# Attention scores in four PSUM banks a head in place of six, maxima over fewer keys, and new due times, in a fused attention, Fourier and MLP kernel

## The chip, the cores and the metric

The kernel runs on one core of one Trainium2 chip. The metric is device time in microseconds of one execution; lower is better.

## The reference

There are 8 batches, 8 heads, 576 positions and 64 dimensions a head. Causal attention with a bias from a cumulative sum comes first, then a Fourier mixing over positions and features, a normalization, and an MLP with a residual:

```python
scores = scale * np.matmul(q, k.transpose(0, 1, 3, 2))
cum = np.cumsum(np.maximum(s, 0.0), axis=-1)
bias = -(cum[:, :, :, None] - cum[:, :, None, :])
scores = np.where(causal, -1000000000.0, scores + np.minimum(bias, 0.0))
attn = exp(scores - max(scores)); attn = attn / (sum(attn) + 1e-09)
x = (attn @ v)                                   # to (8, 576, 512)
u = x + real(fft(fft(x, axis=1), axis=2))
un = (u - mean(u)) / sqrt(var(u) + 1e-06)
out = u + np.maximum(un @ w_ch1, 0.0) @ w_ch2    # 512 -> 2048 -> 512
```

## The kernel before

**Stages.** Attention runs over 32 pairs of heads (8 batches, 4 pairs each; `pair`, `NP` = 32). After the four pairs of a batch its Fourier mixing follows (`folds`, `fourier`), interleaved with later pairs. In the same time the MLP's weights are converted. Then come the normalization and the MLP over nine tiles of 512 tokens: two in plain form (`mlp`), the others in a seven-product form (`fast_tile`, L347).

**One pair.** `high` copies q and k to a high part in the data type fp32r on ScalarE, `low` makes the low parts (VectorE and GpSimd). `maxes` finds each query's greatest score from the high parts alone and writes it as a row beside q, so that the scores' product subtracts it. `scores` makes the score blocks transposed, keys on partitions and queries in the free dimension. `av` multiplies with the values, and with ones for the sums; `recip` and `finish` normalize.

**Scores.** The keys are cut into five chunks of 128, 128, 128, 128 and 64 (`CH`). A key sees the queries from its own position on, so chunk c needs the queries from 128c: 576, 448, 320, 192 and 64 columns, 1600 in all, which lie side by side in the tile `P` (`POFF`, `PW` = 1984 with the unused end). Chunk 0 is cut in two (256 and 320 columns), and chunk 3 is computed over 256 columns, of which the exponential reads the last 192. So a head has six blocks of 256, 320, 448, 320, 256 and 64 columns. Each block (`one`) takes one of three PSUM banks (`ps`, `bufs=3`), gets two matmuls, one with the high parts (L684, `ky` and `qy`) and one with the parts for the correction (L685, `k1` and `q1`), each with its own weight load of 128 columns, and is read by one exponential on ScalarE (L690), which frees the bank. GpSimd then puts zeros above the diagonal: `select` (L709) for the first four chunks at once, behind their five exponentials (`diag`), and a small one (L697) for the fifth chunk, behind its own.

**Maxima.** `maxes` has eight steps a pair. `unit` is the form for the first two blocks of 128 queries: both heads side by side in one bank, 256 keys each (L588), then one bf16 matmul that adds the causal mask for both heads to the 128 columns at `cut` (L590), then one reduce on VectorE over the first `cut + 128` columns of each head (L593). `masked` (L600) and `last` (L624) take the other queries. Their banks are of another ring of three (`psm`).

**Order.** The program writes down each engine's order of instructions. The class `Flow` plans it when the kernel is built. Every piece of work is a generator that yields the engine that it wants next with an estimated cost, the events that it depends on and a ring's slot (a buffer). The planner simulates these engines, and among the pieces that could start within 0.02 us of the earliest it takes the one with the least due time. Due times come from the table `PR`: pair i is due at `D(i)`, which is `T * i` with T = 14.85 plus an offset `d<i>`, and the steps of a pair, the Fourier stages (`fold`, `fou`, `b<n>`, the last batch's `fo2`, `fo3`), the weights (`a0`, `dw`, `w2`, `lw`, `kp`) and the rest of the MLP (`c0`, `ld`) have offsets of their own. For instance the split of weight block f into two parts (L1087) is due at

```python
A0 = O + PR['a0']                        # O = T * 31 - 4
return A0 + 5.5 * f - PR['dw']           # due_w(f)
```

The planner's estimates only set the order; on the chip the engines wait for each other by semaphores.

Of the kernel before, what the change touches and what calls it, by code (L numbers as in the profile page):

```python
# [10 lines left out]
AF = mybir.ActivationFunctionType  # L11
# [18 lines left out]
N1 = 6  # L30
NW = 8
MARGIN = 1.5
PR = {'high': -1.74, 'hstep': 2.12, 'low': -1.84, 'p0': 0.0, 'p1': 0.0, 'p2': 0.0, 'p3': 0.0, 'win': 0.02, 'a0': 32.04, 'ld': 1.38, 'lw': 41.24, 'kp': 22.34, 'dw': 8.84, 'w2': 5.04, 'nf': -0.16, 'c0': 22.43, 'cvs': 7.29, 'lstep': 1.1, 'qs': -2.41, 'mx': -1.37, 'mxh': -6.12, 'mxc': 0.48, 'mt': 6.04, 'sc': -0.62, 'sch': 6.28, 'scs': 0.76, 'sel': 7.33, 'av': 10.36, 'avh': 15.59, 'avk': 4.5, 'rc': -1.89, 'fin': 17.87, 'fold': 4.62, 'fj': 5.3, 'fst': 2.33, 'fou': 7.67, 'gap': 3.41, 'fo2': 37.01, 'fo3': 43.31, 'gap2': 2.05, 'cv': -0.05, 'T': 14.85, 'b7': 5.15, 'd3': -2.77, 'd10': 4.59, 'd29': -1.01, 'd21': 6.35, 'd13': -0.31, 'b2': 0.88, 'd11': 0.25, 'd28': 0.04, 'b5': 0.6, 'd15': -6.3, 'd5': 3.97, 'd27': -0.16, 'd31': 0.19, 'd16': 2.45, 'd18': 1.56, 'd6': 3.13, 'd17': 0.55, 'd7': 0.12, 'd2': -0.15, 'd14': -3.6, 'd0': -1.05, 'd20': 1.74, 'b4': -3.07, 'd22': 3.32, 'd26': -1.87, 'b6': 9.14, 'd25': -1.62, 'b1': 0.96, 'd23': -1.21, 'd30': -4.22, 'd12': -3.32, 'd19': 1.36, 'd24': 4.33, 'd9': -0.04, 'b0': 0.58, 'd8': 0.46, 'd4': 2.24, 'b3': 0.22, 'd1': -0.58}
BACKLOG = 4.0


CH = [(128, 0, 576, 0), (128, 128, 448, 128), (128, 256, 320, 256), (128, 320, 256, 384), (128, 512, 64, 512)]
POFF = [0, 576, 1152, 1728, 1920]
# [4 lines left out]
def fused_kernel(ctx, tc, qkT, vA, sP, wP, tabD, tabS, corr, out):  # L43
    nc = tc.nc
# [6 lines left out]
    ps = ctx.enter_context(tc.tile_pool(name="ps", bufs=3, space=PSUM))  # L51
# [348 lines left out]
    psm = attp_ctx.enter_context(tc.tile_pool(name="psm", bufs=5, space=PSUM))  # L400
# [6 lines left out]
    flow = Flow()  # L407
    rings = {}

    def ring(name, n):  # L410
        if name not in rings:
            rings[name] = Ring(n)
        return rings[name]
# [3 lines left out]
    def ev(*name):  # L417
        return events.setdefault(name, Event())
# [3 lines left out]

    T = PR['T']

    def D(i):
        return T * i + PR.get('d%d' % i, 0.0)
# [144 lines left out]
    def maxes(i):  # L571
        st = sts[i]
        qy, ky = st["qy"], st["ky"]
# [5 lines left out]
        ready = [at(("rows", i), ("k", i, h), ("q", i, h)) for h in range(2)]  # L579

        def unit(c, k0, cut, out, done):


            e, hold = yield pe(2 * mm(256) + (0.0 if cut is None else 0.25), *ready[0], *ready[1], ring=(ring("psm", 3), 1))
            p = psm.tile([128, 512], F32, tag="m", name="pm", bufs=3)
            both = p.rearrange("p (h n) -> p h n", n=256)
            for h in range(2):
                nc.tensor.matmul(both[:, h], qy[:, h, 128 * c:128 * c + 128], ky[:, h, k0:k0 + 256], start=not h, stop=cut is None and h == 1, skip_group_check=True)  # L588
            if cut is not None:
                nc.tensor.matmul(both[:, :, cut:cut + 128], identb, mask2, start=False, stop=True, skip_group_check=True)  # L590
            valid = 256 if cut is None else cut + 128
            e = yield ("DVE", 0.16 + 0.00205 * valid, (e, *free), None)
            nc.vector.tensor_reduce(out=out, in_=both[:, :, 0:valid], axis=AX.X, op=ALU.max)  # L593
            hold.add(e)
            done.add(e)
# [47 lines left out]
        e, hold = yield pe(0.1, ev("max", i), ring=(ring("psm", 3), 1))  # L643
        p = psm.tile([128, 512], F32, tag="m", name="pmt", bufs=3)
        nc.tensor.transpose(out=p[0:9, 0:128], in_=M[:, 0:9], identity=ident)
        ev("moved", i).set(e)
        e, mthold = yield act(128, e, ring=(ring("mt", 2), 2))
# [13 lines left out]
        e = yield ("ACT", 0.74, (), None)  # L661
# [5 lines left out]
    def scores(i):  # L667
        st = sts[i]
        qy, ky, q1, k1 = st["qy"], st["ky"], st["q1"], st["k1"]
        st["P"], st["Phold"] = [], []  # L670
        scored = Last(ev("scored", i), 12)
        for h in range(2):
            _, hold = yield wait(ev("row", i), ev("low", i), ring=(ring("P", 4), 1))
            P = attp.tile([128, PW], F32, tag="P", name="P", bufs=4)
            st["P"].append(P)
            st["Phold"].append(hold)
            diag = Last(Event(), 5)

            def one(h, c, a, n, P, diag):
                nk, q0, nq, qk = CH[c]  # L680
                ksl = slice(128 * c, 128 * c + 128)
                e, hold = yield pe(2 * mm(max(n, 128)), ring=(ring("ps", 3), 1))
                p = bank("ps")
                nc.tensor.matmul(p[:, :n], ky[:, h, ksl], qy[:, h, a:a + n], start=True, stop=False)  # L684
                nc.tensor.matmul(p[:, :n], k1[:, h, ksl], q1[:, h, a:a + n], start=False, stop=True)  # L685
                scored.add(e)
                lo = max(a, qk)
                o = POFF[c] + lo - qk
                e = yield act(a + n - lo, e)
                nc.scalar.activation(P[:, o:o + a + n - lo], p[:, lo - a:n], AF.Exp, scale=0.125)  # L690
                hold.add(e)
                if c < 4:
                    diag.add(e)
                else:
                    e = yield pool_(64, e)
                    d5 = P[:, POFF[4]:POFF[4] + 64]
                    nc.gpsimd.affine_select(out=d5, in_=d5, pattern=[[1, 64]], compare_op=ALU.is_ge, fill=0.0, base=0, channel_multiplier=-1)  # L697
                    ev("P5", i, h).set(e)

            x = 0  # L700
            for c, (nk, q0, nq, qk) in enumerate(CH):
                for a, n in [(0, 256), (256, 320)] if c == 0 else [(q0, nq)]:
                    flow.add(one(h, c, a, n, P, diag), D(i) + PR['sc'] + PR['sch'] * h + PR['scs'] * x)
                    x += 1

            def select(P, diag, h):
                e = yield ("POOL", 0.68, (diag.event,), None)
                d4 = bass.AP(tensor=P.tensor, offset=P.offset, ap=[list(P.ap[0]), [576, 4], [1, 128]])
                nc.gpsimd.affine_select(out=d4, in_=d4, pattern=[[0, 4], [1, 128]], compare_op=ALU.is_ge, fill=0.0, base=0, channel_multiplier=-1)  # L709
                ev("P4", i, h).set(e)  # L710

            flow.add(select(P, diag, h), D(i) + PR['sch'] * h + PR['sel'])
        ev("begun", i).set(ev("row", i))
# [919 lines left out]
def pe(cost, *deps, ring=None):  # L1633
    return "PE", cost, deps, ring


def act(n, *deps, ring=None):
    return "ACT", 0.16 + n * 0.0009, deps, ring
# [26 lines left out]
def mm(n):  # L1665
    return 0.012 + n / 2350
# [146 lines left out]
```

## Time and profile before

| what | us |
|---|---|
| median of 3 runs | 1318.52 (1315.52 to 1319.11) |
| profiled execution, in all | 1313.49 |
| its span, first to last instruction | 1311.8 |
| TensorE busy in the span | 1235.9 |
| VectorE, ScalarE, GpSimd busy | 780.0, 607.2, 551.0 |
| granted TensorE clock, mean | 0.982 of full |

A matmul's row in the profile starts where the record puts it, and its end is modelled; it lasts longer than the time to the next start, because matmuls are pipelined. Weight loads are a row of their own (PEld) and overlap matmuls. A wait is put down to the operation that came last by the profile.

### The profile page before, as it was taken

The numbers are of one execution on the slowest core, as the hardware profiler recorded it, in microseconds if no ns is written. First come the engines' busy times: TensorE is split into PE (matmuls) and PEld (weight loads), VectorE is DVE, ScalarE is ACT, GpSimd is POOL, SyncE is SP. The second block draws the span as 40 slices with busy tenths as digits, with TensorE's granted clock in tenths as the row PEclk, the third lists the DMA queues.
The fourth block names the chain that finished last, engine by engine and source line by source line (L and its number), as shares of the span: only waits on it lengthen the run. The fifth ranks groups of instructions, "written<-read, shape, count | busy, mean of one in ns | idle before, by whom it ended". The sixth has DMA issues, their size and how long they took to land.

```text
span 1311.8 us, 22882 instructions
## 1 busy us (share of the span) xinstructions
PE 1235.9 (94%) x8414; PEld 1031.7 (79%) x8414; DVE 780.0 (59%) x1440; ACT 607.2 (46%) x1388; POOL 551.0 (42%) x569
## 2 busy tenths in 40 slices
PE   3998889899999979899999999999999999999998
PEld 2766667677776757787788888899888988888987
DVE  6566776847678577839757865444454444535323
ACT  2876776667676563425333432333233333333221
POOL 9456676857758675528743502102021021120100
PEclk9999899999999999999999999999999999999999
DMA  8867675646666465277543335244353442533433
GB/s 192 226 183 208 179 204 171 196 118 182 175 167 175 107 210 196 76 245 233 185 152 130 114 121 174 96 145 151 103 173 119 137 154 96 171 118 122 147 102 113
DMA packets 120395, 205.61 MB, mean 157 GB/s; under 512 B 16537, under 2 KB 38457, under 8 KB 120283
## 3 DMA queue, kind: packets, MB, share of 16 engines
q1 hardware_dynamic: 117707, 200.96, 49.1%
q0 software_dynamic: 1712, 2.53, 1.1%
q8 instruction: 66, 1.08, 0.3%
q10 hardware_dynamic: 864, 0.67, 0.2%
q14 instruction: 46, 0.38, 0.1%
HBM read 148.44 MB, written 31.72 MB: 137 GB/s over the span
## 4 chain that ended last, share of the span: by engine, by line
PE 55%; DVE 8%; POOL 3%; issue 3%; DMA 2%; ACT 1%; SPq 0%; POOLq 0%; DVEq 0%; ACTq 0%
PE b L347 20%; PE acc L259 7%; PE acc L258 7%; PE acc L260 7%; PE h L1396 4%; DVE we L88 1%; PE acc L1378 1%; PE acc L1377 1%; PE acc L1379 1%; DVE we L85 1%; PE pav L733 1%; PE pz L926 1%; DVE wl L1087 1%; PE pav L748 1%; DMA w2l<-wD 1%
## 5 line engine op out<-in xcount | busy, mean ns | idle before, releaser
L305 POOL TENSOR_TENSOR w<-w,o 128x512 f32<-128x512 f32 x28 | 37.2, 1338 | 346.5 <-DVE o L301 307.0
L259 PE MATMUL acc<-zh,w2l 128*128 128x512 f32 x452 | 179.3, 397 | 0.0
L258 PE MATMUL acc<-zh,w2h 128*128 128x512 f32 x452 | 178.8, 396 | 0.0
L260 PE MATMUL acc<-zl,w2h 128*128 128x512 f32 x452 | 177.2, 392 | 0.0
L690 ACT ACTIVATE P<-ps 128x320 f32<-128x320 f32 (+4 forms) x384 | 130.1, 393 | 41.3 <-PE ps L685 35.1
L684 PE MATMUL ps<-KQ 128*128 128x256 f32 (+3 forms) x384 | 121.9, 330 | 6.9 <-ACT P L690 6.3
L339 ACT ACTIVATE zh<-cs 128x256 fp32r<-128x256 f32 x112 | 58.8, 525 | 141.6 <-DVE cs L359 86.0
L685 PE MATMUL ps<-Q,K 128*128 128x256 f32 (+3 forms) x384 | 114.9, 312 | 0.0
L340 DVE SCALAR_TENSOR_TENSOR zl<-cs,zh 128x256 fp32r<-128x256 f32 x112 | 66.0, 590 | 69.2 <-ACT zh L339 69.2
L603 DVE CUSTOM_DVE_ANT_0 trash<-pm,amask 128x384 bf16<-128x384 f32 (+1 forms) x128 | 79.1, 618 | 39.4 <-PE pm L600 33.0
L554 POOL TENSOR_TENSOR Q<-qk,Q 64x576 fp32r<-64x576 f32 x64 | 95.2, 1508 | 17.1 <-DMA Q<-KQ 7.5
L347 PEld LDWEIGHTS b<-bh,wh 128*128 128x128 f32 x448 | 83.8, 188 | 22.0 <-DVE cs L359 2.4
L260 PEld LDWEIGHTS acc<-zl,w2h 128*128 128x128 f32 x452 | 85.0, 188 | 19.3 <-DVE zl L340 0.4
L347 PE MATMUL b<-bh,wh 128*128 128x256 f32 x448 | 89.2, 280 | 1.6 <-DVE cs L359 1.6
L684 PEld LDWEIGHTS ps<-KQ 128*128 128x128 f32 x384 | 75.4, 196 | 19.0 <-ACT P L690 14.2
L347 PE MATMUL b<-bh,wl 128*128 128x256 f32 x448 | 90.0, 282 | 0.0
L347 PE MATMUL b<-bl,wh 128*128 128x256 f32 x448 | 89.6, 281 | 0.0
L259 PEld LDWEIGHTS acc<-zh,w2l 128*128 128x128 f32 x452 | 86.3, 191 | 2.6
L733 PE MATMUL pav<-P,va 128*64 128x448 f32 (+3 forms) x640 | 87.3, 419 | 0.0
L258 PEld LDWEIGHTS acc<-zh,w2h 128*128 128x128 f32 x452 | 84.8, 188 | 2.9
L359 DVE TENSOR_TENSOR cs<-cs,b 128x256 f32<-128x256 f32 x56 | 23.5, 420 | 103.9 <-PE b L347 103.2
L733 PEld LDWEIGHTS pav<-P,va 128*64 128x64 f32 x640 | 43.2, 137 | 49.0 <-issue 39.8
(223 smaller groups left out, 3114.3 us busy)
## 6 DMA issues: line engine op xcount, KB each, us to landing
w2h<-w2D SPq DMA_DIRECT2D x128, 256.0 KB
w2l<-w2D SPq DMA_DIRECT2D x128, 256.0 KB
qk<-in_qkT_dram SPq DMA_DIRECT2D x32, 576.0 KB
raw<-in_wP_dram SPq DMA_DIRECT2D x32, 512.0 KB
va<-in_vA_dram SPq DMA_DIRECT2D x32, 320.0 KB
u<-uD SPq DMA_DIRECT2D x10, 1024.0 KB
Q<-KQ SPq DMA_DIRECT2D x32, 288.0 KB
K<-KQ SPq DMA_DIRECT2D x32, 288.0 KB
```

Of the source, the lines that this page charges most:

```text
L258: nc.tensor.matmul(acc[j], a[:, cs], y, start=first, stop=False)
L259: nc.tensor.matmul(acc[j], b[:, cs], y, start=False, stop=False)
L260: nc.tensor.matmul(acc[j], a[:, cs], z, start=False, stop=final)
L339: nc.scalar.activation(y[0][:, at], src, AF.Relu)
L340: nc.vector.scalar_tensor_tensor(out=y[1][:, at], in0=src, scalar=0.0, in1=y[0][:, at].bitcast(F32), op0=ALU.max, op1=ALU.subtract)
L347: nc.tensor.matmul(p[:, 0:256], a[:, j * 128:(j + 1) * 128], b[:, j], start=start and i == 0, stop=i == 5, skip_group_check=not start)
L554: nc.gpsimd.tensor_sub(q1[64:128, h], qk[0:64, h], q1[0:64, h].bitcast(F32))
L603: nc.vector.tensor_tensor_reduce(out=trash[:, 0:n], in0=p[:, 0:n], in1=amask[:, m0:m0 + n], scale=1.0, scalar=NEG, op0=ALU.add, op1=ALU.ma ...
L684: nc.tensor.matmul(p[:, :n], ky[:, h, ksl], qy[:, h, a:a + n], start=True, stop=False)
L685: nc.tensor.matmul(p[:, :n], k1[:, h, ksl], q1[:, h, a:a + n], start=False, stop=True)
L690: nc.scalar.activation(P[:, o:o + a + n - lo], p[:, lo - a:n], AF.Exp, scale=0.125)
L733: nc.tensor.matmul(p[64 * h:64 * h + 64, 0:n], va[:, c, 64 * h:64 * h + 64], P[h][:, o:o + n], start=start, stop=stop)
```

## The change

The six blocks of a head become four banks, each read by one exponential: 512 columns of chunk 0; 64 columns of chunk 0 and 448 of chunk 1; 320 of chunk 2; 192 of chunk 3 and 64 of chunk 4. In a bank with two parts, the two matmuls with the high parts come first and then the two of the correction; only the first matmul of the bank has the start flag. Chunk 3 is now computed over the 192 columns that are read. A head keeps twelve score matmuls. The planner's cost of a part is `max(0.075, mm(n))`, where before it was `mm(max(n, 128))`, with `mm(n) = 0.012 + n / 2350`. The select over the first four chunks waits for all four exponentials, that with the fifth chunk among them.

In `maxes`, a `unit` with a mask computes `cut + 128` keys in place of 256: 128 for the first 128 queries, 256 as before for the second. The reduce reads the same columns as before.

In the table `PR`, `T` stays at 14.85 and so do `mx`, `mxh`, `mxc`, `avh`, `avk`, `fin`, `win`; most of the others move. The pairs' offsets move by up to 3.3 (`d31` 0.19 to -3.13, `d30` -4.22 to -1.62, `d26` -1.87 to -4.25). At the end: `a0` 32.04 to 34.2, `dw` 8.84 to 3.9, `w2` 5.04 to 6.08, `c0` 22.43 to 23.96, `lw` 41.24 to 39.91, `kp` 22.34 to 23.74, `fo2` 37.01 to 34.88, `fo3` 43.31 to 44.13, `gap2` 2.05 to 1.17, `fj` 5.3 to 2.61.

```diff
@@ the table PR (values above)
...
@@ -581,11 +581,12 @@
         def unit(c, k0, cut, out, done):
 
 
-            e, hold = yield pe(2 * mm(256) + (0.0 if cut is None else 0.25), *ready[0], *ready[1], ring=(ring("psm", 3), 1))
+            n = 256 if cut is None else cut + 128
+            e, hold = yield pe(2 * mm(n) + (0.0 if cut is None else 0.25), *ready[0], *ready[1], ring=(ring("psm", 3), 1))
             p = psm.tile([128, 512], F32, tag="m", name="pm", bufs=3)
             both = p.rearrange("p (h n) -> p h n", n=256)
             for h in range(2):
-                nc.tensor.matmul(both[:, h], qy[:, h, 128 * c:128 * c + 128], ky[:, h, k0:k0 + 256], start=not h, stop=cut is None and h == 1, skip_group_check=True)
+                nc.tensor.matmul(both[:, h, 0:n], qy[:, h, 128 * c:128 * c + 128], ky[:, h, k0:k0 + n], start=not h, stop=cut is None and h == 1, skip_group_check=True)
             if cut is not None:
                 nc.tensor.matmul(both[:, :, cut:cut + 128], identb, mask2, start=False, stop=True, skip_group_check=True)
             valid = 256 if cut is None else cut + 128
@@ -668,40 +669,40 @@
         st = sts[i]
         qy, ky, q1, k1 = st["qy"], st["ky"], st["q1"], st["k1"]
         st["P"], st["Phold"] = [], []
-        scored = Last(ev("scored", i), 12)
+        scored = Last(ev("scored", i), 8)
         for h in range(2):
             _, hold = yield wait(ev("row", i), ev("low", i), ring=(ring("P", 4), 1))
             P = attp.tile([128, PW], F32, tag="P", name="P", bufs=4)
             st["P"].append(P)
             st["Phold"].append(hold)
-            diag = Last(Event(), 5)
-
-            def one(h, c, a, n, P, diag):
-                nk, q0, nq, qk = CH[c]
-                ksl = slice(128 * c, 128 * c + 128)
-                e, hold = yield pe(2 * mm(max(n, 128)), ring=(ring("ps", 3), 1))
+            diag = Last(Event(), 4)
+
+            def one(h, parts, P, diag):
+
+
+                total = sum(n for _, _, n in parts)
+                e, hold = yield pe(2 * sum(max(0.075, mm(n)) for _, _, n in parts), ring=(ring("ps", 3), 1))
                 p = bank("ps")
-                nc.tensor.matmul(p[:, :n], ky[:, h, ksl], qy[:, h, a:a + n], start=True, stop=False)
-                nc.tensor.matmul(p[:, :n], k1[:, h, ksl], q1[:, h, a:a + n], start=False, stop=True)
+                for x, (kk, qq) in enumerate(((ky, qy), (k1, q1))):
+                    o = 0
+                    for y, (c, a, n) in enumerate(parts):
+                        nc.tensor.matmul(p[:, o:o + n], kk[:, h, 128 * c:128 * c + 128], qq[:, h, a:a + n], start=x == y == 0, stop=x == 1, skip_group_check=True)
+                        o += n
                 scored.add(e)
-                lo = max(a, qk)
-                o = POFF[c] + lo - qk
-                e = yield act(a + n - lo, e)
-                nc.scalar.activation(P[:, o:o + a + n - lo], p[:, lo - a:n], AF.Exp, scale=0.125)
+                c, a, _ = parts[0]
+                o = POFF[c] + a - CH[c][3]
+                e = yield act(total, e)
+                nc.scalar.activation(P[:, o:o + total], p[:, 0:total], AF.Exp, scale=0.125)
                 hold.add(e)
-                if c < 4:
-                    diag.add(e)
-                else:
+                diag.add(e)
+                if parts[-1][0] == 4:
                     e = yield pool_(64, e)
                     d5 = P[:, POFF[4]:POFF[4] + 64]
                     nc.gpsimd.affine_select(out=d5, in_=d5, pattern=[[1, 64]], compare_op=ALU.is_ge, fill=0.0, base=0, channel_multiplier=-1)
                     ev("P5", i, h).set(e)
 
-            x = 0
-            for c, (nk, q0, nq, qk) in enumerate(CH):
-                for a, n in [(0, 256), (256, 320)] if c == 0 else [(q0, nq)]:
-                    flow.add(one(h, c, a, n, P, diag), D(i) + PR['sc'] + PR['sch'] * h + PR['scs'] * x)
-                    x += 1
+            for x, parts in enumerate((((0, 0, 512),), ((0, 512, 64), (1, 128, 448)), ((2, 256, 320),), ((3, 384, 192), (4, 512, 64)))):
+                flow.add(one(h, parts, P, diag), D(i) + PR['sc'] + PR['sch'] * h + PR['scs'] * 1.5 * x)
 
             def select(P, diag, h):
                 e = yield ("POOL", 0.68, (diag.event,), None)
```

## Rows read from the trace of the kernel before

**Rows 1.** The profile's page: busy time of TensorE (its share of the span, its instructions), and, of the 40 equal slices of the span, TensorE's busy tenths and the clock that it was granted, in tenths of full speed.

```profile
PE 1235.9 (94%) x8414; PEld 1031.7 (79%) x8414; DVE 780.0 (59%) x1440; ACT 607.2 (46%) x1388; POOL 551.0 (42%) x569
...
PE   3998889899999979899999999999999999999998
...
PEclk9999899999999999999999999999999999999999
```

**Rows 2.** Busy time by engine in three stretches of the span, with the number of instructions in brackets; behind the engines the granted TensorE clock, the busy share of the DMA engines and GB/s. The first column is the stretch (us from the span's start), the second its length.

```profile
40.00:480.00 440.00, 412.56 (x3713) 312.49 (x3712) 305.78 (x677) 309.98 (x760) 302.90 (x340) 0.98 0.62 175
480.00:650.00 170.00, 152.96 (x692) 125.48 (x691) 127.86 (x157) 73.87 (x137) 102.55 (x77) 0.95 0.57 191
650.00:1312.00 662.00, 652.86 (x3956) 580.87 (x3954) 325.68 (x566) 209.68 (x466) 112.96 (x97) 1.00 0.40 132
```

**Rows 3.** The timeline of TensorE's matmuls from 233.9 to 235.5 us: start, us from the first start to the last (modelled) end, line, operation, out<-in, weights and columns, number. L684 and L685 are the two products of a score block.

```profile
234.01 0.28 PE L684 MATMUL ps<-KQ 128*128 128x256 f32 x1
...
234.24 0.31 PE L684 MATMUL ps<-KQ 128*128 128x320 f32 x1
...
234.54 0.36 PE L684 MATMUL ps<-KQ 128*128 128x448 f32 x1
...
234.94 0.40 PE L624 MATMUL pm<-KQ,q 128*128 128x256 f32 x2
```

**Rows 4.** The same view from 219.3 to 221.2 us: a matmul of 512 columns (L600, maxima) and the start of what follows it.

```profile
219.74 0.39 PE L600 MATMUL pm<-KQ 128*128 128x512 f32 x1
219.97 1.36 PE L973 MATMUL py<-ssin,zs 96*128 96x290 f32 x9
```

**Rows 5.** The same view from 220.8 to 223.2 us: the end of a head's scores with its two matmuls of 64 columns, and what follows them.

```profile
221.28 0.28 PE L685 MATMUL ps<-Q,K 128*128 128x256 f32 x1
221.40 0.19 PE L684 MATMUL ps<-KQ 128*128 128x64 f32 x1
221.43 0.28 PE L685 MATMUL ps<-Q,K 128*128 128x64 f32 x1
221.54 0.54 PE L624 MATMUL pm<-KQ,q 128*128 128x320 f32 x2
221.91 0.57 PE L600 MATMUL pm<-KQ 128*128 128x384 f32 x2
```

**Rows 6.** The timeline of TensorE's weight loads (PEld) over the same stretch.

```profile
221.28 0.19 PEld L684 LDWEIGHTS ps<-KQ 128*128 128x128 f32 x1
221.40 0.19 PEld L685 LDWEIGHTS ps<-Q,K 128*128 128x128 f32 x1
221.51 0.30 PEld L624 LDWEIGHTS pm<-KQ,q 128*128 128x128 f32 x2
```

**Rows 7.** The timeline of matmuls from 223.7 to 224.95 us: a unit of the maxima, its two products (L588) and its mask (L590).

```profile
223.79 0.40 PE L588 MATMUL pm<-KQ 128*128 128x256 f32 x2
224.03 0.28 PE L590 MATMUL pm<-mask,identb 128*128 128x256 bf16 x1
```

**Rows 8.** Groups of instructions by line and form from 50 to 450 us: weight loads of these products and of the mask. Columns: line, engine, operation, out<-in, shapes, number | busy us, mean ns of one | idle us before them.

```profile
L588 PEld LDWEIGHTS pm<-KQ 128*128 128x128 f32 x115 | 18.2, 190 | 3.6 <-DVE Mx L603 2.3 <-ACT zs L932 0.8
...
L590 PEld LDWEIGHTS <-identb 128*128 128x128 bf16 x58 | 5.6, 96 | 2.6
```

**Rows 9.** The same view, the exponentials (L690) by their columns.

```profile
L690 ACT ACTIVATE P<-ps 128x320 f32<-128x320 f32 x114 | 49.8, 437 | 12.9 <-PE ps L685 10.9 <-ACT mt L649 1.7
...
L690 ACT ACTIVATE P<-ps 128x448 f32<-128x448 f32 x57 | 31.1, 546 | 5.4 <-PE ps L685 5.2
...
L690 ACT ACTIVATE P<-ps 128x256 f32<-128x256 f32 x56 | 21.6, 385 | 9.0 <-PE ps L685 7.2 <-PE pm L600 0.9
...
L690 ACT ACTIVATE P<-ps 128x192 f32<-128x192 f32 x57 | 18.8, 330 | 7.3 <-PE ps L685 6.4 <-PE pm L624 0.8
...
L690 ACT ACTIVATE P<-ps 128x64 f32<-128x64 f32 x56 | 12.5, 224 | 4.8 <-PE ps L685 3.8 <-PE pm L600 0.8
```

**Rows 10.** The timeline of ScalarE from 241.0 to 243.5 us: five exponentials in a row (256, 320, 448, 320 and 192 columns; the row names the first).

```profile
241.59 1.74 ACT L690 ACTIVATE P<-ps 128x256 f32<-128x256 f32 x5 [0.16 <-PE ps L685]
```

**Rows 11.** Who waited for whom from 40 to 480 us, TensorE's matmuls: us in total, times, longest.

```profile
PE ps L684 <- ACT P L690: 6.3, 8, 1.6
PE pav L740 <- POOL P L709: 4.8, 12, 0.7
PE pm L600 <- DVE Mx L593: 3.6, 5, 2.6
```

**Rows 12.** The same, TensorE's weight loads.

```profile
PEld ps L684 <- ACT P L690: 13.8, 31, 2.0
```

**Rows 13.** Busy time by engine in slices of 10 us, at the end of attention (columns as in rows 2).

```profile
480.00:490.00 10.00, 3.81 (x21) 3.52 (x20) 10.00 (x11) 6.23 (x14) 9.02 (x6) 0.77 0.61 209
490.00:500.00 10.00, 7.43 (x32) 5.58 (x31) 10.00 (x18) 6.74 (x12) 6.83 (x4) 0.84 0.62 212
```

**Rows 14.** The chain that ended last from 465 to 545 us, its longer pieces in order of time: start, us, what.

```profile
487.08 0.59 DVE wl L1087
...
488.94 0.49 DVE wl L1087
...
496.03 1.36 DVE wl L1087
...
500.35 2.44 PE h L1396 x6
```

More of the change, by code (lines that the diff above doesn't have):

```diff
@@ L32 @@
 MARGIN = 1.5
-PR = {'high': -1.74, 'hstep': 2.12, 'low': -1.84, 'p0': 0.0, 'p1': 0.0, 'p2': 0.0, 'p3': 0.0, 'win': 0.02, 'a0': 32.04, 'ld': 1.38, 'lw': 41.24, 'kp': 22.34, 'dw': 8.84, 'w2': 5.04, 'nf': -0.16, 'c0': 22.43, 'cvs': 7.29, 'lstep': 1.1, 'qs': -2.41, 'mx': -1.37, 'mxh': -6.12, 'mxc': 0.48, 'mt': 6.04, 'sc': -0.62, 'sch': 6.28, 'scs': 0.76, 'sel': 7.33, 'av': 10.36, 'avh': 15.59, 'avk': 4.5, 'rc': -1.89, 'fin': 17.87, 'fold': 4.62, 'fj': 5.3, 'fst': 2.33, 'fou': 7.67, 'gap': 3.41, 'fo2': 37.01, 'fo3': 43.31, 'gap2': 2.05, 'cv': -0.05, 'T': 14.85, 'b7': 5.15, 'd3': -2.77, 'd10': 4.59, 'd29': -1.01, 'd21': 6.35, 'd13': -0.31, 'b2': 0.88, 'd11': 0.25, 'd28': 0.04, 'b5': 0.6, 'd15': -6.3, 'd5': 3.97, 'd27': -0.16, 'd31': 0.19, 'd16': 2.45, 'd18': 1.56, 'd6': 3.13, 'd17': 0.55, 'd7': 0.12, 'd2': -0.15, 'd14': -3.6, 'd0': -1.05, 'd20': 1.74, 'b4': -3.07, 'd22': 3.32, 'd26': -1.87, 'b6': 9.14, 'd25': -1.62, 'b1': 0.96, 'd23': -1.21, 'd30': -4.22, 'd12': -3.32, 'd19': 1.36, 'd24': 4.33, 'd9': -0.04, 'b0': 0.58, 'd8': 0.46, 'd4': 2.24, 'b3': 0.22, 'd1': -0.58}
+PR = {'high': -1.77, 'hstep': 1.91, 'low': -1.84, 'p0': 0.0, 'p1': 0.0, 'p2': 0.0, 'p3': 0.0, 'win': 0.02, 'a0': 34.2, 'ld': 1.79, 'lw': 39.91, 'kp': 23.74, 'dw': 3.9, 'w2': 6.08, 'nf': -0.44, 'c0': 23.96, 'cvs': 7.26, 'lstep': 1.1, 'qs': -2.68, 'mx': -1.37, 'mxh': -6.12, 'mxc': 0.48, 'mt': 6.6, 'sc': -0.62, 'sch': 6.32, 'scs': 0.77, 'sel': 6.52, 'av': 12.16, 'avh': 15.59, 'avk': 4.5, 'rc': -2.02, 'fin': 17.87, 'fold': 4.78, 'fj': 2.61, 'fst': 2.56, 'fou': 7.33, 'gap': 3.3, 'fo2': 34.88, 'fo3': 44.13, 'gap2': 1.17, 'cv': -0.05, 'T': 14.85, 'b7': 5.0, 'd3': -2.65, 'd10': 4.03, 'd29': 0.58, 'd21': 6.61, 'd13': -0.31, 'b2': 0.88, 'd11': 0.67, 'd28': 0.14, 'b5': 0.6, 'd15': -7.32, 'd5': 3.97, 'd27': -1.59, 'd31': -3.13, 'd16': 1.88, 'd18': 0.53, 'd6': 2.03, 'd17': 0.55, 'd7': 0.12, 'd2': -0.13, 'd14': -2.56, 'd0': -0.82, 'd20': 1.28, 'b4': -3.05, 'd22': 3.32, 'd26': -4.25, 'b6': 8.31, 'd25': -0.43, 'b1': 0.75, 'd23': -0.61, 'd30': -1.62, 'd12': -3.94, 'd19': 1.0, 'd24': 4.07, 'd9': 0.62, 'b0': 0.58, 'd8': 0.86, 'd4': 1.59, 'b3': 0.22, 'd1': -0.58}
 BACKLOG = 4.0
```

## The prediction

> **What bounds the kernel now.** I read the engine table and the 40 slices first [rows 1], then the stages [rows 2], then single matmuls with their weight loads [rows 3 to 8], the exponentials [rows 9, 10], the waits [rows 11, 12] and the end of attention [rows 13, 14]. In rows 1 see that TensorE is busy 94% of the span at a clock near full. In rows 2 see three stages: attention with the Fourier work between 40 and 480 us, the passage to the MLP up to 650, and the MLP, where TensorE has nothing left over and where the change edits no operation. In attention TensorE is busy 412.6 of 440 us (27.4 idle), VectorE 305.8, ScalarE 310.0, GpSimd 302.9. So attention is bound by TensorE, with short waits on all the others, and what a head costs TensorE is the first question; what ScalarE gains is worth something only where TensorE waits for it.
>
> **What a matmul of a score costs.** The price is read as the time from one start to the next. Two matmuls of 256 columns take 0.23 us, two of 320 take 0.30, two of 448 take 0.40 [rows 3]; one of 512 takes 0.23 [rows 4]. The narrow ones are the trap. The two of 64 columns seem to start 0.03 us apart [rows 5], but look at their weight loads: the load for the second begins at 221.40, when the first matmul starts, and the load for the matmul after it begins only at 221.51 [rows 6]. A load of 128 columns thus takes 0.11 us and the next cannot begin before the matmul that uses the present one has started. The third matmul shows it: from 221.40 to 221.91 there are two of 64 and two of 320 columns, 0.51 us, of which the two wide ones are 0.30, so the narrow ones take 0.21 together. A matmul costs the larger of its columns and the next load, and below about 256 columns it is the load: 0.11 us.
>
> The Trainium skill says two things on this that point apart. "TensorE: Matmul & The Clock Gate", section LDWEIGHTS, gives columns of weights / 1.2 ns, 107 ns for 128, which speaks against narrow matmuls; the rows above agree. Its section "Back-to-back issue gap" lists 1 to 64 columns at about 60 cycles, by which an added 64-column matmul would be nearly free; the rows disagree, and by it the sum below would be that of the second rival.
>
> **The change, part by part.**
>
> *Score matmuls.* A head has twelve before and twelve after (each with its own weight load, so no load is saved). Before, in pairs: 256, 320, 448, 320, 256, 64 columns: 0.23 + 0.30 + 0.40 + 0.30 + 0.23 + 0.22 = 1.68 us. After: 512, 64, 448, 320, 192, 64: 0.46 + 0.22 + 0.40 + 0.30 + 0.22 + 0.22 = 1.82 us. The columns fall from 1664 to 1600 per operand, yet TensorE works 0.14 us longer, since a third of the matmuls are now no wider than a load. 64 heads: +9.0 us. No row has 192 columns in this data type. Between the neighbours, 64 (0.11) and 256 (0.115), nothing lower or higher is expected; were it to run like four times its columns it would cost 0.32, a rival below. All of it lies on TensorE, so the cover is only TensorE's idle time. I let 0.8 of a change in TensorE's work reach the end (94% busy, less a little for waits whose cause doesn't move with TensorE), bounds 0.5 and 1.
>
> *Maxima.* For the first 128 queries two matmuls of 256 columns take 0.24 us up to the mask [rows 7]. After, they have 128 columns: the first still costs the second's load, 0.11; the second is followed by the bf16 mask, whose load is short (96 against 190 ns for the same 128 columns [rows 8]), so it may run at its columns, 0.06. That is -0.07 us for each of 32 head pairs, -2.2 us (bounds: 0 if neither gains, -3.7 if both halve). The reduce on VectorE already reads 128 columns of each head, so it stays.
> Both together: +6.8 us of TensorE, times 0.8: **+5.4** (bounds +2.6, with nothing but half passed on and the larger gain, and +9.0).
>
> *Exponentials.* Six instructions of 385, 437, 546, 437, 330 and 224 ns [rows 9] are 2.36 us a head; the four, with 512 columns put at 546 + 64 x 0.85 = 600 ns by the step from 320 to 448, are 600 + 600 + 437 + 385 = 2.02. 0.34 us a head is 21.6 us of ScalarE in busy time, but five in a row take 1.74 us [rows 10] where their means add to 2.13: each overlaps the next by 0.10, so a run of them saves only some 0.13 a head, 9 us. ScalarE has 130 us to spare in attention [rows 2]: as work this counts 0, hidden by TensorE; were that cover gone it would be worth the 9 to 21.6.
>
> *The ring of three banks.* This is where the gain can come from. TensorE fills a bank in 1.68 / 6 = 0.28 us; ScalarE, back to back, empties one in 2.36 / 6 - 0.10 = 0.29 and has casts to do between. So TensorE runs into a full ring: its weight loads for the scores waited for an exponential 31 times, 13.8 us [rows 12], 0.45 us each (TensorE's own line shows 6.3 us in 8 of them [rows 11], its modelled tails covering the rest). After, a bank is filled in 0.455 and emptied in 0.505 - 0.10 = 0.41: the order is turned round, and three banks hold 1.37 us of TensorE's work in place of 0.84, 0.53 us more than before and more than the mean wait. Most of these waits should go, the longest (2.0 us) in part. Bounds 0 and -13.8; I take **-8.0**. Late next is the select ahead of the value products.
>
> *Selects.* The select of the four diagonals waited for five exponentials and now waits for all four, so the last bank, with keys 512 to 575, is added to its wait; behind it on GpSimd stands the small select, which waits for that bank too. TensorE's wait for the select is 4.8 us in all [rows 11]. A head's last exponential ends earlier by the ScalarE saving, and the sixth one's time is added: **0**, bounds +4.8 and -4.8. No DMA is added or moved by this.
>
> *Due times.* They change only what the planner puts first, and it prices a narrow matmul at 0.075 us, the load at 0.11 being unknown to it. The clearest shift is at the end: the splits of the first weights are due 2.16 + 4.94 = 7.1 us later against the norms. The chain there has three splits (0.59, 0.49, 1.36 us) among the norm's subtractions ahead of the MLP's first long run of products [rows 14], while TensorE idles 8.8 us in the 20 us [rows 13]. I take the three splits' **-2.4**; bounds +8.8, a second such hole, and -8.8, the hole gone.
>
> Sum: +5.4 - 8.0 + 0 - 2.4 = **-5.0 us**. The profiled execution (span 1311.8, 1313.49 in all) lies 5.0 below the median of the runs, 1318.52; the durations are of that execution, and I set the difference on the median: 1318.5 - 5.0 = 1313.5.
>
> **The rivals.**
> *Slower: weights in place of waits.* The 0.14 us a head is paid in full and the ring gives nothing, because ScalarE's casts and copies, not the count of banks, hold it up, or because a 512-column bank simply waits longer for both its ends. For it: TensorE is the fullest engine, and its own line shows only 6.3 us of such waits [rows 11]. Against: the 13.8 us of [rows 12]. +6.8 gives 1325.3. It decides (slower by over 0.3%, 4 us, about what a measurement of this kernel can tell from no change) where the ring gives back under 2.8 us.
> *Columns alone set the price.* Then TensorE gains: 128 columns a head at 2.4 GHz are 0.053 us, 3.4 us over 64 heads, and the maxima 3.4: -6.8 x 0.8 = -5.4, with the other terms 1302.7. Against it are the load starts of [rows 6].
> *The terms cancel.* 5.4 from TensorE, half of the ring's term (-4), nothing from the due times: 1319.9. For it: most of the 27.4 us idle stands in waits that the change doesn't touch [rows 11].
> *Narrow columns run at a quarter rate.* 192 columns then take 0.32 in place of 0.11: 128 such matmuls, +27 us, with the sum 1340. Against it: the matmul behind a 64-column one is recorded 0.03 us later [rows 5], what 64 columns take at full rate.
>
> **How the numbers follow.** Forecast 0.36 and columns alone 0.06 are faster, 0.42; cancelling 0.31 is the same; weights in place of waits 0.24 and quarter rate 0.03 are slower, 0.27. The range takes in columns alone at its low end and the slower rival at its high end: 1302 to 1326; outside lie the quarter rate, larger gains from the due times and a second hole, under 0.2 together.
>
> **What would show it.** Loads of the 64- and 192-column matmuls 0.11 us apart and TensorE's score matmuls 1.8 us a head: the first term. 256 exponentials, those of 512 columns near 0.60 us, and weight loads waiting for an exponential less than 6 us in all: the ring. TensorE's idle time from 480 to 500 us under 6.4: the due times. The prediction is wrong if the waits for exponentials stay above 11 us, if loads stand closer than 0.08 us, or if attention ends more than 5 us off where the sum of the first two terms (-2.6) puts it.

## The result, and the profile after

The changed kernel takes 1328.06 us (median of 5 runs, 1324.08 to 1331.94); the kernel before took 1317.2 us in the runs of that comparison (5 runs, 1312.92 to 1319.11). The ratio is 1.0087, with a 95% interval of 1.0063 to 1.0111: 0.9% slower, some 11.5 us, where 5 us of gain were forecast, and 2 us outside the range. The times and ratios of this text leave out two executions at a far lower granted clock, 1385.53 us (0.84) of the kernel before and 1712.64 us (0.66) of the version merge34 below. The profiled execution has a span of 1328.5 us, 16.7 above that of before; it is 2 us above its own median, as the one of before was some 4 us below its own.

The page of the changed kernel, as in [rows 1]:

```profile
span 1328.5 us, 22753 instructions
...
PE 1246.7 (94%) x8414; PEld 1035.9 (78%) x8414; DVE 771.7 (58%) x1440; ACT 598.3 (45%) x1260; POOL 549.4 (41%) x569
...
PE   3988988999999888899999999999999999999998
...
PEclk9999998999999898899999999999999999999999
```

TensorE is busy 10.8 us longer and idle 5.9 us longer (81.8 against 75.9 us): both parts count. The clock line has four 8s, where before it had one. The stages, as in [rows 2]:

```profile
40.00:480.00 440.00, 407.29 (x3558) 306.90 (x3558) 292.38 (x664) 292.70 (x614) 293.58 (x328) 0.97 0.61 169
480.00:650.00 170.00, 152.61 (x780) 122.52 (x780) 121.09 (x160) 78.09 (x151) 97.25 (x81) 0.95 0.58 191
650.00:1329.00 679.00, 669.09 (x4025) 593.64 (x4023) 337.46 (x575) 215.23 (x476) 126.83 (x107) 1.00 0.41 133
```

Attention is not over at 480 us: the last value product ends at 496.9 us, against 477.3 before. So 19.7 us are lost in attention and about 3 come back later; the MLP, where no operation was edited, is not where to look.

One head's scores, the matmuls and then the weight loads (columns as in [rows 3] and [rows 6]; a row with x2 holds both parts of a bank and is named after the first):

```profile
290.69 0.40 PE L689 MATMUL ps<-KQ 128*128 128x512 f32 x1
290.93 0.40 PE L689 MATMUL ps<-Q,K 128*128 128x512 f32 x1
291.16 0.48 PE L689 MATMUL ps<-KQ 128*128 128x64 f32 x2
291.48 0.48 PE L689 MATMUL ps<-Q,K 128*128 128x64 f32 x2
291.79 0.31 PE L689 MATMUL ps<-KQ 128*128 128x320 f32 x1
291.94 0.31 PE L689 MATMUL ps<-Q,K 128*128 128x320 f32 x1
292.09 0.27 PE L646 MATMUL pmt<-ident,Mx 128*9 128x128 f32 x1
292.11 0.39 PE L689 MATMUL ps<-KQ 128*128 128x192 f32 x2
292.34 0.39 PE L689 MATMUL ps<-Q,K 128*128 128x192 f32 x2
292.56 0.42 PE L589 MATMUL pm<-KQ 128*128 128x128 f32 x2
```

```profile
290.70 0.19 PEld L689 LDWEIGHTS ps<-Q,K 128*128 128x128 f32 x1
290.93 0.42 PEld L689 LDWEIGHTS ps<-KQ 128*128 128x128 f32 x2
291.27 0.40 PEld L689 LDWEIGHTS ps<-Q,K 128*128 128x128 f32 x2
291.59 0.19 PEld L689 LDWEIGHTS ps<-KQ 128*128 128x128 f32 x1
...
292.09 0.30 PEld L689 LDWEIGHTS ps<-KQ 128*128 128x128 f32 x2
292.31 0.30 PEld L689 LDWEIGHTS ps<-Q,K 128*128 128x128 f32 x2
292.53 0.30 PEld L589 LDWEIGHTS pm<-KQ 128*128 128x128 f32 x2
292.81 0.10 PEld L591 LDWEIGHTS <-identb 128*128 128x128 bf16 x1
```

Read the loads first. They stand 0.11 us apart from 292.09 to 292.53 (a row x2 of 0.30 holds two loads of 0.19, the second 0.11 later), where 192, 64, 192 and 64 columns are multiplied: 192 columns also cost a load and no more. The head begins at 290.69 and its last matmul ends 0.11 us after 292.53, with a transposition of 0.11 us in between (L646, where another step of the plan was due): 1.84 us, where 1.82 was forecast and 1.68 before. This head is no exception: in the stretches at the higher clock, the distance from load to load has a median of 0.11 us over all heads for 64 columns and for 192. The last two rows show the maxima: the second load of L589 starts 0.11 us behind 292.53, and the mask's load 0.17 us behind that.

The exponentials by their columns, as in [rows 9], and TensorE's waits and its weight loads' waits between 40 and 480 us, as in [rows 11] and [rows 12]:

```profile
L695 ACT ACTIVATE P<-ps 128x512 f32<-128x512 f32 x110 | 63.8, 596 | 24.9 <-PE ps L689 21.4 <-ACT mt L650 0.9 <-PE pm L591 0.8
...
L695 ACT ACTIVATE P<-ps 128x320 f32<-128x320 f32 x55 | 24.0, 437 | 0.6 <-PE ps L689 0.5
...
L695 ACT ACTIVATE P<-ps 128x256 f32<-128x256 f32 x55 | 21.1, 384 | 9.6 <-PE ps L689 6.6 <-PE pm L591 1.6 <-PE pm L601 0.8
```

```profile
PE pav L741 <- POOL P L710: 10.1, 6, 3.5
PE ps L689 <- ACT P L695: 4.7, 5, 1.8
```

```profile
PEld ps L689 <- ACT P L695: 7.2, 9, 2.1
```

The exponentials cost what was worked out (596 ns for 512 columns; 600 forecast), and the loads' wait for them falls from 13.8 to 7.2 us. But the wait of the value products for the select rises from 4.8 to 10.1 us.

### The profile page after: what moved, and what is told of

Same layout as the page of the kernel before. It is cut to its first block, busy times and chain, and to the rows that moved or that the text cites. A ratio compares the mean times of both kernels' runs of the same rounds, so it can differ in the third digit from the quotient of the medians.

```text
span 1328.5 us, 22753 instructions
## 1 busy us (share of the span) xinstructions
PE 1246.7 (94%) x8414; PEld 1035.9 (78%) x8414; DVE 771.7 (58%) x1440; ACT 598.3 (45%) x1260; POOL 549.4 (41%) x569
## 4 chain that ended last, share of the span: by engine, by line
PE 65%; DVE 8%; POOL 4%; DMA 3%; issue 3%; ACT 2%; SPq 0%; ACTq 0%; POOLq 0%; DVEq 0%
PE b L347 20%; PE acc L259 7%; PE acc L258 7%; PE acc L260 7%; PE h L1397 4%; PE ps L689 3%; PE pav L734 3%; PE pav L749 2%; PE pz L927 1%; DVE we L88 1%; PE py L963 1%; PE acc L1379 1%; PE acc L1380 1%; PE acc L1378 1%; PE py L974 1%
## 5 line engine op out<-in xcount | busy, mean ns | idle before, releaser
L695 ACT ACTIVATE P<-ps 128x512 f32<-128x512 f32 (+2 forms) x256 | 118.5, 503 | 43.0 <-PE ps L689 36.0
L689 PE MATMUL ps<-KQ 128*128 128x64 f32 (+4 forms) x384 | 104.6, 328 | 5.5 <-ACT P L695 4.7
L554 POOL TENSOR_TENSOR Q<-qk,Q 64x576 fp32r<-64x576 f32 x64 | 94.7, 1499 | 27.5 <-DMA Q<-KQ 19.7
L689 PE MATMUL ps<-Q,K 128*128 128x64 f32 (+4 forms) x384 | 102.2, 324 | 0.0
L689 PEld LDWEIGHTS ps<-KQ 128*128 128x128 f32 x384 | 71.0, 196 | 15.5 <-ACT P L695 7.2
```

The lines of the kernel that those rows point to most:

```text
L554: nc.gpsimd.tensor_sub(q1[64:128, h], qk[0:64, h], q1[0:64, h].bitcast(F32))
L689: nc.tensor.matmul(p[:, o:o + n], kk[:, h, 128 * c:128 * c + 128], qq[:, h, a:a + n], start=x == y == 0, stop=x == 1, skip_group_check=True)
L695: nc.scalar.activation(P[:, o:o + total], p[:, 0:total], AF.Exp, scale=0.125)
```

## The experiments

Two theories went in. **Weights**: the loss is the price of the narrow matmuls, each as long as the next weight load. **Order**: the loss is the new order of the instructions, whatever they are. Each time is a median beside runs of the kernel before on the same chip, whose medians were 1317.06 us (the runs up to max128), 1316.65 (four_kept, five_kept, merge34, jitter) and 1316.6 (the other four). Differences in us are the ratio's share of 1317 us.

**due_only and ops_only: one half of the change each.** The first is the kernel before with the line `PR = ...` of the changed one, the second the reverse:

```diff
 # due_only: operations of before
-PR = {'high': -1.74, 'hstep': 2.12, ...
+PR = {'high': -1.77, 'hstep': 1.91, ...
 # ops_only: operations of the change
-PR = {'high': -1.77, 'hstep': 1.91, ...
+PR = {'high': -1.74, 'hstep': 2.12, ...
```

> The kernel before with the changed kernel's due times alone; every operation as before. Weights theory (narrow matmuls that last as long as the next weight load cost the 11 us): 0 to +3 us against before. Order theory (the new plan's order costs them, whatever the operations): +8 to +12 us.

Measured 1334.31 us, ratio 1.0141 (1.0116 to 1.0167): +18.6 us.

> The changed kernel with the due times of before: four banks, 128 keys for the first queries, old table. Weights theory: +5 to +10 us against before. Order theory: -3 to +3 us, if the operations are neutral and the old table suits them.

Measured 1364.04 us, ratio 1.0350 (1.0327 to 1.0373): +46 us. Neither theory had that. Each half alone is slower than both together, and the new table takes back 35 of the 46 us that the new operations cost under the old one. It looks as if each table serves only the operations that it was made for; how the tables were made is not on record. So the halves can't be added, and to price the operations the order must be held.

**split512, max128 and split448: operations at a held order.** The planner is told the blocks and costs of before, so that every engine keeps its order and only the shapes differ.

```diff
 # split512 (split448: 448 and 128, told the same)
-for a, n in [(0, 256), (256, 320)] if c == 0 else [(q0, nq)]:
+for a, n in [(0, 512), (512, 64)] if c == 0 else [(q0, nq)]:
-e, hold = yield pe(2 * mm(max(n, 128)), ring=(ring("ps", 3), 1))
+plan = {(0, 0): 256, (0, 512): 320}.get((c, a), n)
+e, hold = yield pe(2 * mm(max(plan, 128)), ring=(ring("ps", 3), 1))
-e = yield act(a + n - lo, e)
+e = yield act(plan if c == 0 else a + n - lo, e)
 # max128
-nc.tensor.matmul(both[:, h], ..., ky[:, h, k0:k0 + 256], ...)
+n = 256 if cut is None else cut + 128
+nc.tensor.matmul(both[:, h, 0:n], ..., ky[:, h, k0:k0 + n], ...)
```

> The kernel before with chunk 0 cut into 512 and 64 columns in place of 256 and 320, still six banks and six exponentials; the planner is told the costs of before, so every engine's order stays the same. Two more matmuls a head are narrower than a weight load: by the weight-load starts 0.46 + 0.22 in place of 0.23 + 0.30 us a head, +9.6 us of TensorE, of which 0.8 reach the end. Weights theory: +6 to +10 us. Order theory, or a price by columns alone: within 2 us of before.

Measured 1323.49 us, ratio 1.0050 (1.0034 to 1.0066): +6.6 us (6.4 by the medians).

> The kernel before with chunk 0 cut into 448 and 128 columns in place of 256 and 320, six banks, order of before (the planner is told the costs of before). A matmul costs the larger of its columns and the next weight load: 0.40 + 0.22 in place of 0.23 + 0.30 us a head, +0.09, times 64 heads +5.8 us of TensorE and +4 to +5 in the time, a little less than split512's +6.4. Columns alone: 0. Narrow columns at a quarter rate (128 columns last 0.21): 0.40 + 0.43, +19 us.

Measured 1318.82 us, ratio 1.0019 (0.9999 to 1.0038): +2.5 us, less than expected and not told from none, far from the +19 of a quarter rate.

> The kernel before with 128 keys for the maxima of the first 128 queries; the planner is told the cost of before, so the order stays the same. Weights theory: the two matmuls take 0.17 in place of 0.24 us, -2.2 us of TensorE, -1.8 us in the time. A price by columns alone: -3.4 of TensorE, -2.7. Order theory: 0. If a matmul of 128 columns ran at a quarter of the rate: +5 or more.

Measured 1315.61 us, ratio 0.9995 (0.9979 to 1.0010): -0.7 us, not told from none; nothing of a quarter rate here either.

The page's span and busy times, split512 and then split448, and the timeline of matmuls in a head of split512:

```profile
span 1319.5 us, 22879 instructions
...
PE 1244.2 (94%) x8414; PEld 1033.1 (78%) x8414; DVE 785.1 (60%) x1440; ACT 609.2 (46%) x1388; POOL 550.0 (42%) x569
```

```profile
span 1315.4 us, 22885 instructions
...
PE 1242.4 (94%) x8414; PEld 1034.8 (79%) x8414; DVE 779.0 (59%) x1440; ACT 609.0 (46%) x1388; POOL 552.1 (42%) x569
```

```profile
236.92 0.40 PE L684 MATMUL ps<-KQ 128*128 128x512 f32 x1
237.16 0.39 PE L685 MATMUL ps<-Q,K 128*128 128x512 f32 x1
237.38 0.19 PE L684 MATMUL ps<-KQ 128*128 128x64 f32 x1
237.41 0.27 PE L685 MATMUL ps<-Q,K 128*128 128x64 f32 x1
237.52 0.45 PE L684 MATMUL ps<-KQ 128*128 128x448 f32 x1
237.81 0.36 PE L685 MATMUL ps<-Q,K 128*128 128x448 f32 x1
```

With the order held, TensorE is busy 8.3 us longer in split512 and 6.5 in split448 (9.6 and 5.8 expected), and in split512 it is idle as long as before (75.3 against 75.9 us): the loss there is work and no wait. In the timeline the two matmuls of 64 columns are recorded 0.03 us apart, as in [rows 5], and what they really cost shows behind them: the first of 448 columns starts 0.29 us ahead of its partner, where its columns alone make 0.20. The split of 512 and 64 columns, with no other change, costs 6.6 us: the weights theory's price is real, and it is not the whole 11.5. split448 alone wouldn't show it, since its interval takes in no loss at all.

**four_kept, five_kept and merge34: the banks at a held order.** Here the planner sees the six blocks of before; the first column of the table stands for a block in the plan, the second for what is issued at its place (the edit is shortened). In the traces of these three runs, of the three above and of merge34max below, the other instructions of TensorE, VectorE, ScalarE and GpSimd, without the score products and their exponentials, stand in the same sequence as in the kernel before.

```diff
+# four_kept (with max128): all operations of the change
+BANKS = {(0,0): ((0,0,512),), (0,256): (), (1,128): ((0,512,64),(1,128,448)),
+         (2,256): ((2,256,320),), (3,320): ((3,384,192),(4,512,64)), (4,512): ()}
+# five_kept: as four_kept, but
+#        (3,320): ((3,384,192),), (4,512): ((4,512,64),)
+# merge34 (without max128): blocks of before, but
+#        (3,320): ((3,320,256),(4,512,64)), (4,512): ()
-nc.tensor.matmul(p[:, :n], ky[:, h, ksl], qy[:, h, a:a + n], start=True, stop=False)
-nc.tensor.matmul(p[:, :n], k1[:, h, ksl], q1[:, h, a:a + n], start=False, stop=True)
+parts = BANKS[(c, a)]      # matmuls and one exponential as in the change, if any
```

> All operations of the changed kernel (four banks, four exponentials, 128 keys) in the order of before: the planner is told the six blocks and costs of before, and the other work keeps its place on every engine. If the operations cost what split512 and max128 showed and the ring gives nothing: +5 us against before (6.4 for the narrow matmuls of 64 columns, under 1 for 192, -1.5 for the maxima). If the ring and the shorter exponentials give back the forecast 8 us: -3. If the late last bank holds up the selects as in ops_only (waits of the value products for the select 17.0 against 4.8 us): +10 to +15. Whatever this is below the changed kernel's +11 us is the order's part.

Measured 1321.68 us, ratio 1.0036 (1.0020 to 1.0053): +4.7 us. All operations of the change, in the order of before, cost 4.7 us. The changed kernel has the same operations and +11.5, so 6.8 us are the order's; with the errors of both put together, 3 to 11. The same operations stand in ops_only too, under the same table as here: there the planner saw four blocks, re-planned everything and lost 46 us, so some 41 us of that are the order's.

> As four_kept, but chunks 3 and 4 keep a bank and an exponential each (192 and 64 columns): five banks, five exponentials, and the select of the four diagonals doesn't wait for the fifth chunk. If the merged last bank's select costs time, this is 3 to 8 us faster than four_kept. If the ring is what counts, it is 1 to 3 us slower than four_kept.

Measured 1324.15 us, ratio 1.0059 (1.0039 to 1.0078): +7.8 us, the opposite of what the select's cost would do: the merged last bank is worth 2.5 us by the medians and 3.1 by the ratios, though the two intervals overlap.

> The kernel before with chunks 3 and 4 in one bank with one exponential, all twelve matmuls with the columns of before (256 of chunk 3, of which 192 are read), in the order of before. TensorE's work is unchanged. The ring's gain alone: -2 to -4 us. The select's cost alone: +2 to +6 us.

Measured 1314.17 us, ratio 0.9980 (0.9963 to 0.9997): -2.6 us. Without a further narrow matmul, one bank and one exponential less seem to be a small gain; the interval ends just below none.

The waits between 40 and 480 us, TensorE's and then its loads', in four_kept and then in five_kept (L754 is the first value product, L692 the score products, L702 the exponential, L723 the select there):

```profile
PE pav L754 <- POOL P L723: 8.5, 13, 1.4
PE ps L692 <- ACT P L702: 4.8, 7, 1.2
```

```profile
PEld ps L692 <- ACT P L702: 7.3, 9, 1.5
```

```profile
PE ps L692 <- ACT P L702: 7.4, 11, 2.8
PE pav L754 <- POOL P L723: 5.5, 9, 1.2
```

```profile
PEld ps L692 <- ACT P L702: 12.2, 21, 3.1
```

In four_kept the loads' wait for exponentials is 7.3 us, 6.5 less than before [rows 12]; with chunk 4 in a bank of its own it is 12.2. On the matmuls' own lines the wait for exponentials falls by 1.5 us (6.3 to 4.8) and the wait for the select rises by 3.7 (4.8 to 8.5 [rows 11]; 5.5 in five_kept, where the select doesn't stand behind a merged last bank). So waits at the ring do go, but others come in their place. TensorE's idle time as a whole is what it was: 44.0 us in four_kept between 40 and 700 us, 44.5 before (rows below).

**jitter, jitter2 and told: how much an order can cost.** The operations are untouched and only the plan is nudged (edits shortened).

```diff
 # jitter (jitter2: 0.3 * (-1) ** (i // 2))
-return T * i + PR.get('d%d' % i, 0.0)
+return T * i + PR.get('d%d' % i, 0.0) + 0.3 * (-1) ** i
 # told: the changed kernel
-e, hold = yield pe(2 * sum(max(0.075, mm(n)) for _, _, n in parts), ...)
+e, hold = yield pe(2 * sum(max(0.11, mm(n)) for _, _, n in parts), ...)
```

> The kernel before with each pair's due time moved by 0.3 us, up for even pairs and down for odd ones; operations as before. It shows what another order of the same work costs, where the changed table's is +17. If the table of before stands at a narrow optimum: +5 us or more. If only the changed table is poor: within 3 us.

Measured 1344.97 us, ratio 1.0213 (1.0188 to 1.0238): +28 us.

> The kernel before with the due times of pairs moved by 0.3 us in another pattern (two pairs up, two down). If the table of before stands at a narrow optimum, as jitter showed: +10 to +30 us against before. If jitter was one unlucky order: within 5 us.

Measured 1321.92 us, ratio 1.0040 (1.0021 to 1.0058): +5.3 us, less than expected, and still not the order of before.

> The changed kernel with its own table, its planner told 0.11 us for a narrow score matmul in place of 0.075; operations as changed. If the plan is poor because it prices the narrow matmul too low: -3 to -7 us against the changed kernel (+5 to +8 against before). If any order that the table was not fitted to is worse, as in jitter: +10 us or more above the changed kernel (+20 or more against before).

Measured 1348.31 us, ratio 1.0233 (1.0201 to 1.0265): +31 us, 19 above the changed kernel. Told the price that the loads show, the plan gets worse. That doesn't clear the wrong price: the table stayed, and jitter shows that a new order under an old table can cost this much by itself.

Where does an order's cost show? The stretch from 40 to 700 us, columns as in [rows 2], in turn for the kernel before, four_kept, the changed kernel, due_only, told, jitter and ops_only:

```profile
40.00:700.00 660.00, 615.51 (x4619) 478.55 (x4619) 463.28 (x875) 398.75 (x922) 424.52 (x434) 0.97 0.59 177
```

```profile
40.00:700.00 660.00, 616.05 (x4602) 477.10 (x4601) 461.76 (x871) 390.63 (x795) 425.34 (x434) 0.97 0.59 176
```

```profile
40.00:700.00 660.00, 609.39 (x4547) 469.05 (x4548) 445.63 (x866) 386.57 (x790) 419.08 (x433) 0.96 0.59 175
```

```profile
40.00:700.00 660.00, 600.84 (x4505) 459.46 (x4505) 445.04 (x860) 391.17 (x907) 414.49 (x430) 0.95 0.59 173
```

```profile
40.00:700.00 660.00, 602.88 (x4463) 458.98 (x4464) 439.18 (x848) 377.83 (x777) 413.44 (x427) 0.94 0.58 170
```

```profile
40.00:700.00 660.00, 595.83 (x4482) 459.01 (x4471) 452.09 (x855) 389.08 (x905) 414.02 (x429) 0.95 0.59 172
```

```profile
40.00:700.00 660.00, 591.18 (x4434) 450.96 (x4435) 433.78 (x841) 378.43 (x775) 406.99 (x423) 0.93 0.57 168
```

Take TensorE's idle time (660 less its busy time) and what the clock held back (660 times 1 less the granted clock; the two levels are 1.2 and 2.4 GHz, so a mean of 0.97 is 6% of the time at the lower one):

| kernel | idle, us | held back, us | sum against before | span against before |
|---|---|---|---|---|
| before | 44.5 | 19.8 | 0 | 0 |
| four_kept | 44.0 | 19.8 | -0.5 | +3.7 |
| changed | 50.6 | 26.4 | +12.7 | +16.7 |
| due_only | 59.2 | 33.0 | +27.9 | +26.9 |
| told | 57.1 | 39.6 | +32.4 | +35.8 |
| jitter | 64.2 | 33.0 | +32.9 | +31.2 |
| ops_only | 68.8 | 46.2 | +50.7 | +45.0 |

The clock has two digits, so its column is good to some 3 us, each row is one execution, and time idle at the lower clock counts in both columns. Even so the sum follows the span within 6 us in these seven rows, while the spans differ by up to 45. The sum holds only waits and clock, no work: in four_kept, in the order of before, it is nil, and the span's 3.7 us are work. A poorer order goes with more idle time and with a lower granted clock, though not in one proportion: told has less idle time than due_only and more held back.

Up to the end of attention the same can be read for the kernel before, four_kept and the changed kernel, each to its last value product:

```profile
40.00:477.30 437.30, 410.26 (x3699) 310.66 (x3698) 304.33 (x675) 307.33 (x754) 302.30 (x339) 0.98 0.62 176
```

```profile
40.00:482.10 442.10, 413.83 (x3700) 311.87 (x3698) 305.19 (x675) 300.34 (x630) 303.01 (x339) 0.98 0.62 174
```

```profile
40.00:496.90 456.90, 420.99 (x3702) 314.72 (x3702) 300.75 (x677) 301.94 (x636) 305.16 (x343) 0.97 0.61 169
```

TensorE does the same number of matmuls in each, within three. In four_kept attention ends 4.8 us later than before, with 1.2 us more idle time and the same clock to two digits. In the changed kernel it ends 19.6 us later: 8.9 us more are idle, some 5 more are held back (13.7 against 8.7), and the rest, some 6 and good to 3, is near the 3.6 that four_kept loses in work. No one wait carries the idle time: in the changed kernel, up to 480 us, the wait for the select is 10.1 us against 8.5 in four_kept, that for exponentials 4.7 against 4.8, and the rest is in waits of under 4 us in total each.

**merge34max: the two small gains together.** merge34 with the edit of max128.

> merge34 (chunks 3 and 4 in one bank and one exponential, columns as before) together with the 128 keys of max128, in the order of before: what is gained without a further narrow score matmul. If both small gains are real and add: -3 to -5 us against before. If they were noise: 0.

Measured 1314.82 us, ratio 0.9987 (0.9969 to 1.0004): -1.7 us, not told from none and less than the sum of the two. merge34 is the one version whose interval lies wholly on the faster side, by 0.2% and barely; among twelve versions that is weak. Both it and this are some 13 us faster than the change.

## Why the prediction was wrong

**The score matmuls: right.** Forecast: 0.14 us a head and +9.0 us of TensorE, 0.8 of it in the end, 7.2. The changed kernel's head takes 1.84 us against 1.82 forecast, and split512, the same two narrow matmuls a head at a held order, costs +6.6 us. The larger of the columns and the next load was the right price; 192 columns cost one load. The rival in which columns alone set the price is out: split512 has the columns of before and is slower. (The prediction calls a third of the matmuls after the change no wider than a load; by its own prices it is half, two of 192 columns and four of 64 among twelve, and its sum has them so.) The Trainium skill's "TensorE: Matmul & The Clock Gate", section LDWEIGHTS, gives a load as its columns / 1.2 ns, from which 107 ns is an estimate for 128 columns; the loads here stand 0.11 us apart. The table of its section "Back-to-back issue gap", which the prediction set against this, is by that section's own words for single matmuls: "In a real kernel — a stream of `LDWEIGHTS → MATMUL` pairs — the per-MM spacing is set by *both* ops". The prediction took the two sections to point apart; they don't.

**The maxima: right on TensorE, not settled in the time.** Forecast: 0.17 in place of 0.24 us. In max128's trace, at the higher clock, the second load of such a pair and the mask's load stand 0.17 us apart (median of 32 pairs), 0.235 before. In the time -1.8 was forecast in the end; measured is -0.7 with an interval of -2.8 to +1.3.

**The ring of three banks: too large, the second step that failed.** The wait fell nearly as forecast (13.8 to 7.2 us, where under 6 was named; 6.5 less in four_kept), but the time did not follow by 8 us. four_kept less split512 and max128 leaves 4.7 - 6.6 + 0.7 = -1.2 us for all that merging the banks gives; with the errors of the three that is -5 to +2.5, and -8 lies outside. merge34 has -2.6. The prediction took a wait removed for time gained. In its place the wait for the select rose by 3.7 us, the term that I had put at 0, and TensorE's idle time as a whole stayed (44.0 against 44.5 us).

**The due times: the step that failed.** I took -2.4 us from three splits at the end, with bounds of 8.8 on either side, and left out what the order of all the other instructions would cost; they "change only what the planner puts first". That is just what costs: the table alone is +18.6 us on the operations of before, a nudge of 0.3 us on every pair is +28 us or +5 us by its pattern, and in the changed kernel the order is +6.8 us over the order of before. A change in the blocks' number and costs re-plans everything behind it (ops_only, +46 us where four_kept has +4.7), so the change had an order term even without a new table, and mine was read off three rows at the end of attention [rows 14]. The hole there [rows 13] can't be compared slice by slice, since attention now runs through it; but from 480 to 700 us TensorE idles 17.9 us, and 17.1 before, so the 2.4 did not come. The prediction had named an end of attention more than 5 us off as a sign against it: it is 19.7 us later than before, and 22 from where the prediction put it.

The sum as the runs have it: +6.6 - 0.7 - 1.2 + 6.8 = +11.5 us. It closes by construction, as the last two terms are differences of runs. Against the forecast of -5.0 that is 16.5 us: 9.2 from the due times, 6.8 from the ring and 0.5 from the matmuls. The rival that came true in its sign is "weights in place of waits"; its price, 6.8 us with nothing back, was near that of the operations alone (4.7), and its condition, a ring that gives back under 2.8 us, was met by the -1.2, though not clear of the noise. It lacked the order's part, which is why the range ended 2 us short.

What stays open is which property of an order makes it good, and why the clock is lower under a poorer one: the runs show that the loss lies in many small waits and in the granted clock, not which choices of the plan cause them. Nor is it shown where the 6.8 us of the changed order come from, the new table or the four blocks that the planner sees: ops_only and due_only change one of them each, and their costs don't add.

## What to carry to other kernels

Price a matmul with its own weights as the larger of its columns and the next load (0.11 us for 128 columns of weights here), and count how many narrow ones a regrouping makes, before counting saved evacuations. Where a fitted plan sets the order, price operations with the order held, by telling the planner the old costs; otherwise a re-plan can move the time by several times what the operations do (46 us against 4.7 here). Give any re-plan a range as wide as what a nudge of the same plan does.

## What the runs showed that I had not expected

Moving each pair's due time by 0.3 us of a 14.85 us period, with every operation the same, costs 2.1% in one pattern (jitter) and 0.4% in another (jitter2). And narrow matmuls that are recorded 0.03 us apart show their price on the matmul behind them: 0.29 us in place of 0.20 in split512.
